# Re-sequencing the first hundred microseconds of a fused attention and MoE kernel

## Chip, cores, metric

The kernel runs on one NeuronCore of one Trainium2 chip. The metric is device microseconds of one execution. The profile's own span is 1.7 to 2.5 us shorter than the time of the same execution (median 1.8). Ratios come from timed runs. A ratio is the mean time of one kernel's fast runs over that of the other's in the same rounds, so it is not quite the ratio of the medians that are quoted beside it. A run is called slow when it is over 1.5% above the fastest run of the same kernel in its job; all others are called fast. The clock is the share of full speed that PE was granted, as the profile records it.

Engines are named as the profile names them: PE is TensorE, DVE is VectorE, ACT is ScalarE, POOL and SP issue the DMAs, and PEld is the loading of PE's weights. Tiles whose names begin with `ps` lie in PSUM; every matmul in the profiles writes to one of them.

## The reference

Sparse attention (8 global keys, 96 local keys, exponential distance bias) for 4 batches, 8 heads, 768 positions, head size 64. The heads are concatenated and go through a two-layer MLP, which the program calls MoE:

```python
scores = q @ k.T / 8 + bias          # keep = global or (0 <= rel < 96)
a = softmax(where(keep, scores, -1e9))
x = concat_heads(a @ v)              # 3072 x 512
h = x @ w_in                         # 512 -> 2048
g = s * relu(h)**2 + b
out = g @ w_out                      # 2048 -> 512, float32
```

The constant `b` goes through `w_out` as b times the column sums of `w_out`. The kernel builds those sums with 15 DVE additions ("wsum").

## The kernel before

Work is cut into 12 granules of 256 positions, each with four units of two heads. A unit has `stage_S` (scores on PE, exp on ACT, mask multiplication on DVE) and `stage_A` (attention times v on PE, division by the row sum on DVE, into `xn`). A granule then has x transposed, the first MoE matmul in eight groups (`p1`) and the second in two row blocks (`p2`). The program is scheduled by hand (`manual_schedule`): it emits each engine's instructions in the order in which they are to run, so the order of emission is the schedule. From granule 3 on, a `step` interleaves two units with MoE work of earlier granules. The part ahead of it is written out by hand. In the profiles below, `pt` holds the exp of the scores, which the mask multiplies, and `koff` and `voff` are copies of k and v, shifted by one block and with the global keys put in, for every granule but the first of a batch.

```python
def qk_by_pe(j, h2s, evac):                # q and k of one pair of head pairs in ONE PSUM tile
    for h2 in h2s:
        ps = ps_h.tile([P, 2, GB, 2, P], BF16, tag="psh")      # tag psh has 3 buffers
        ...                                # 8 transposes, n=0 is k, n=1 is q
        for n in range(2):
            evac[n](dst, ps[:, n])         # DVE, or one DVE and one ACT
def x_by_pe(j): ...                        # 8 transposes, one ACT copy of 128x1024
def x_by_dma(j):                           # from granule X_PE on
    for i in range(GB): nc.sync.dma_start_transpose(t[:, :, ...], xn[j][:, i, :])
def warm(n): ...                           # n matmuls of zeros that fill PE's time
# ---- loads: v0, (k,q)1, v1, w_in in quarters, w_out in quarters, granules 2 and 3
warm(11); cast_first(0); qk_by_pe(0, [0]); ...
s0[1](); warm(4); stage_A(0); s1 = scores(1); stage_A(1, ps_h); run(s1); warm(2)
stage_A(2); stage_A(3, ps_h); qk_by_pe(1, evac=both); x_by_pe(0)
... run(scores(2)); make_voff(1); warm(6)
run(p1[0][0:2]) ...                        # first w_in matmul
... run(p1[1][4:8])                        # granules 0 and 1 through the first MoE matmul
for qt in range(4):                        # second MoE matmul of granule 0
    for tb in range(GB): p2_mm(0, tb, qt * nq, (qt + 1) * nq)
    run(sums[qt : qt + 1])                 # wsum additions, the other 11 follow later
p2_mm(1, 0, 0, FC // 2); run(sums[4:8]); qk_by_pe(2, [0], evac=both) ...
# ... [cut: attention of granule 2 and 3]
step(6, [], p1[2][0:2], sums[9:10] + p1[2][2:4] + sums[10:11]) ...
```

The softmax here doesn't subtract the row's maximum and nothing guards it: scores larger than these inputs give would overflow.

Of the kernel before, what the change touches and what calls it, by code (L numbers as in the profile page):

```python
# [17 lines left out]
def kernel(  # L18
# [13 lines left out]
    nc = tc.nc  # L32
# [35 lines left out]
    QK_PE = 4  # L68
    X_PE = 4
# [27 lines left out]
    def load_granule(j):  # L97
        b, g = divmod(j, NGR)
        t = nat_tile(j)
        for i in range(GB):  # L100
            for n in range(2):
                nc.gpsimd.dma_start(t[:, n, i, :, :], rows_of(srcs[n], b, g * GB + i))  # L102
        load_v(j)
# [78 lines left out]
    load_granule(1)  # L182
    for i in range(4):
        load_w_in(i, 4)
# [11 lines left out]
    for h in range(H):  # L196
        slope = float(2.0 ** (-8.0 * (h + 1) / H))
        nc.scalar.activation(tmpl[:, h, 0:3, :], base[:], ACT.Exp, scale=slope)
# [5 lines left out]
    def cast_first(h2):  # L204
        hs = slice(h2 * H // 2, (h2 + 1) * H // 2)
        for n in range(2):
            nc.vector.tensor_copy(
                nat[0][:, n, :, hs, :],
                first_f32[h2, n][:].rearrange("p h (s d) -> p s h d", s=GB),
            )  # L210
# [25 lines left out]
    def qk_by_pe(j, h2s=range(HP // 2), evac=(nc.vector.tensor_copy, nc.vector.tensor_copy)):  # L236
        b, g = divmod(j, NGR)
        t = qk_tile(b)
        for h2 in h2s:
            ps = ps_h.tile([P, 2, GB, 2, P], BF16, name="ps_t", tag="psh")  # L240
            for n in range(2):
                for i in range(GB):
                    for c in range(2):
                        hp = 2 * h2 + c
                        nc.tensor.transpose(
                            ps[:, n, i, c, :],
# [3 lines left out]
            for n in range(2):  # L250
                dst = t[:, n, g * GB : (g + 1) * GB, 2 * h2 : 2 * h2 + 2, :]
                if j == 0:
# [3 lines left out]
                        ps[:, n].rearrange("p s c (b m) -> p c b m s", b=GB),  # L256
                    )
                else:
                    evac[n](dst, ps[:, n])  # L259
# [12 lines left out]
    def make_koff(j):  # L272
        b, g = divmod(j, NGR)
        if g == 0:
# [3 lines left out]
        ko = work.tile([P, GB, HP, P], BF16, name="koff", tag="koff", bufs=2)  # L278
        nc.vector.tensor_copy(ko[:], t[:, 0, r0 : r0 + GB, :, :])
        nc.vector.tensor_copy(  # L280
            ko[:, :, :, 0:NG],
            t[:, 0, 0, :, 0:NG].unsqueeze(1).to_broadcast((P, GB, HP, NG)),
        )
        koff[j] = ko
# [15 lines left out]
    def stage_S(u):  # L300
# [18 lines left out]
        for oc, kt, qt in plan:  # L319
            for hi in range(2):  # L320
                rows = slice(hi * D, (hi + 1) * D)
                nc.tensor.matmul(  # L322
                    ps[:, hi, oc * P : (oc + 1) * P],
                    lhsT=kt[rows],
                    rhs=qt[rows],
                    start=True,
                    stop=True,
                )

        def post():  # L330
            nc.scalar.activation(pt[:, :, 0:ncol], ps[:, :, 0:ncol], ACT.Exp, scale=QSCALE)  # L331
            c0 = 0 if first else 1
# [4 lines left out]
        return [post]  # L337
# [43 lines left out]
    def x_by_pe(j):  # L381
        t = xT_tile(j)
        ps = ps_h.tile([P, KC, GT], BF16, name="ps_x", tag="psh")
        for kc in range(KC):
            for i in range(GB):
                nc.tensor.transpose(
                    ps[:, kc, i * P : (i + 1) * P],
                    xn[j][:, i, kc * P : (kc + 1) * P],
                    ident_bf[:],
                )  # L390
        nc.scalar.copy(t[:], ps[:])
# [37 lines left out]
    def split_wsum():  # L429
        nc.vector.tensor_copy(hi[:], wsum[:])  # L430
# [55 lines left out]


# [9 lines left out]
    def scores(s):  # L497
        posts = []
        if s < NU // 2:
            for u in (2 * s, 2 * s + 1):  # L500
                posts += stage_S(u)
        return posts
# [9 lines left out]
    def step(s, c0, c1, c2):  # L512
# [6 lines left out]
        if not last:  # L519
# [6 lines left out]
        stage_A(2 * s + 1)  # L526
# [8 lines left out]
    warm(11)  # L535
    cast_first(0)
    qk_by_pe(0, [0])
    cast_first(1)
    s0 = scores(0)
    s0[0]()  # L540
    qk_by_pe(0, [1], evac=both)
    s0[1]()
    warm(4)
    stage_A(0)
    s1 = scores(1)
    stage_A(1, ps_h)
    run(s1)
# [3 lines left out]
    qk_by_pe(1, evac=both)  # L551
    x_by_pe(0)
    template_rest()
    make_koff(1)
    run(scores(2))
    make_voff(1)
    warm(6)
    run(p1[0][0:2])
    s3 = scores(3)
    stage_A(4)  # L560
    stage_A(5)
    run(s3)
    run(p1[0][2:4])
    stage_A(6)
    run(p1[0][4:5])
    stage_A(7)
    run(p1[0][5:6])
    x_by_pe(1)
    run(p1[0][6:7])
    run(p1[1][0:4])  # L570
    run(p1[0][7:8])
    run(p1[1][4:8])
    nq = FC // 4
    for qt in range(4):
        for tb in range(GB):
            p2_mm(0, tb, qt * nq, (qt + 1) * nq)
        run(sums[qt : qt + 1])
    load_granule(4)
    load_granule(5)
    for tb in range(GB):  # L580
        p2_hold(0, tb)


    p2_mm(1, 0, 0, FC // 2)
    run(sums[4:8])
    qk_by_pe(2, [0], evac=both)
    p2_mm(1, 0, FC // 2, FC)
    qk_by_pe(2, [1], evac=both)
    p2_hold(1, 0)
    make_koff(2)  # L590
    run(scores(4))
    p2_mm(1, 1, 0, FC // 2)
    make_voff(2)
    s5 = scores(5)
    stage_A(8)
    stage_A(9, ps_h)
    run(s5)
    p2_mm(1, 1, FC // 2, FC)
    p2_hold(1, 1)
    stage_A(10)  # L600
    qk_by_pe(3, evac=both)
    stage_A(11)
    run(scores(6))
    run(sums[8:9])
    x_by_pe(2)
    qk_by_dma(4)
    step(6, [], p1[2][0:2], sums[9:10] + p1[2][2:4] + sums[10:11])
    qk_by_dma(5)
    step(7, p1[2][4:5], sums[11:12] + p1[2][5:7], p1[2][7:8] + sums[12:13])
    hold2 = [lambda t=t: (p2_mm(2, t), p2_hold(2, t)) for t in range(GB)]  # L610
    step(8, hold2[0:1], sums[13:14] + p1[3][0:2], sums[14:15] + p1[3][2:4])
    split_wsum()
    step(9, hold2[1:2], [emit_bvec] + p1[3][4:6], p1[3][6:8])
    late = [lambda j=j, t=t: p2_late(j, t) for j in range(3) for t in range(GB)]
# [47 lines left out]
```

## Time and profile before

| | before |
|---|---|
| time | 230.25 us (228.81 to 230.26, 3 runs), 230.0 with a fourth |
| span in the profile | 228.1 us |
| PE busy | 207.7 us |
| first w_in matmul | 18.66 us |
| first second-MoE matmul | 36.87 us |
| scores of step 13 begin | 107.74 us |

From the page of the kernel before: span, PE's busy line, and the rows of the 40 equal slices for PE, for the granted clock and for DMA (tenths).

```profile
span 228.1 us, 4835 instructions
...
PE 207.7 (91%) x1954; PEld 140.9 (62%) x1977; DVE 142.9 (63%) x345; ACT 114.3 (50%) x170; POOL 67.6 (30%) x85
...
## 2 busy tenths in 40 slices
PE   7558899978798899799899999999999999999993
...
PEclk9999999999999999999999999999999999999999
DMA  6999999999999999899999935135130220311102
```

PE is close to full in the later slices, and the clock is full in all of them. The reserve is in the first half. The table of stretches shows it. Its columns are the stretch in us, its length, then busy us and instruction count of PE, PEld, DVE, ACT and POOL, then granted clock, DMA share and GB/s.

```profile
...
0.00:17.30 17.30, 11.13 (x120) 6.55 (x121) 11.40 (x33) 10.26 (x18) 15.01 (x25) 1.00 1.45 166
17.30:36.90 19.60, 17.90 (x196) 14.90 (x192) 11.47 (x30) 13.47 (x20) 7.01 (x8) 1.00 1.40 198
36.90:60.70 23.80, 20.42 (x197) 11.50 (x198) 15.63 (x34) 11.77 (x17) 14.04 (x16) 1.00 2.62 143
60.70:107.70 47.00, 43.19 (x444) 30.58 (x447) 38.28 (x94) 27.31 (x40) 30.58 (x35) 1.00 1.84 150
107.70:220.00 112.30, 110.85 (x990) 75.66 (x1003) 64.57 (x156) 51.50 (x77) 0.94 (x2) 1.00 0.49 83
```

From 107.7 to 220 us PE works 110.85 of 112.3 us. In the four stretches before it PE is idle for 6.2, 1.7, 3.4 and 3.8 us. The list of PE's waits up to 113 us says on whom it waits (us in total, times, longest).

```profile
PE ps_av L361 <- DVE xn L370: 4.1, 6, 1.1
PE ps_s L322 <- DVE koff L280: 2.1, 2, 1.2
PE ps_s L322 <- DVE qk L254: 1.4, 1, 1.4
PE ps_av L361 <- DVE voff L295: 1.3, 2, 0.7
...
PE ps_1731 L407 <- DMA xT<-xn: 0.7, 1, 0.7
...
```

ACT's waits up to 62 us have these two lines on the shared transpose tile:

```profile
ACT qk L259 <- DVE qk L259: 6.9, 4, 2.8
...
ACT qk L254 <- DVE qk L254: 1.3, 1, 1.3
```

ACT waited for DVE to finish its half of the same tile. Last, the SP queue's timeline with the DMA transposes (start, us on the queue, what):

```profile
...
103.70 2.95 SPq L396 DMA_TRANSPOSE xT<-xn  x2
107.41 6.41 SPq L266 DMA_TRANSPOSE qk<-nat  x4
```

The pair at 103.70 us is x, and one group of PE waited 0.7 us for it (the last line of PE's waits above).

### The profile page before, as it was taken

The numbers are of one execution on the slowest core, as the hardware profiler recorded it, in microseconds if no ns is written. First come the engines' busy times: TensorE is split into PE (matmuls) and PEld (weight loads), VectorE is DVE, ScalarE is ACT, GpSimd is POOL, SyncE is SP. The second block draws the span as 40 slices with busy tenths as digits, with TensorE's granted clock in tenths as the row PEclk, the third lists the DMA queues.
The fourth block names the chain that finished last, engine by engine and source line by source line (L and its number), as shares of the span: only waits on it lengthen the run. The fifth ranks groups of instructions, "written<-read, shape, count | busy, mean of one in ns | idle before, by whom it ended". The sixth has DMA issues, their size and how long they took to land.

```text
span 228.1 us, 4835 instructions
## 1 busy us (share of the span) xinstructions
PE 207.7 (91%) x1954; PEld 140.9 (62%) x1977; DVE 142.9 (63%) x345; ACT 114.3 (50%) x170; POOL 67.6 (30%) x85
## 2 busy tenths in 40 slices
PE   7558899978798899799899999999999999999993
PEld 3346786445575657477567657756765776675841
DVE  3696736638697886979567666557585674342421
ACT  7558564255977466327374455347446532340610
POOL 8973346982199560567100000000000000000000
PEclk9999999999999999999999999999999999999999
DMA  6999999999999999899999935135130220311102
GB/s 170 136 187 206 207 204 156 154 150 111 148 135 154 124 153 87 104 198 269 194 148 170 142 67 99 71 61 126 49 82 14 68 72 3 92 46 49 46 0 92
DMA packets 106934, 27.06 MB, mean 119 GB/s; under 512 B 97696, under 2 KB 103840, under 8 KB 106912
## 3 DMA queue, kind: packets, MB, share of 16 engines
q0 software_dynamic: 74944, 13.11, 81.1%
q1 hardware_dynamic: 31968, 13.64, 31.4%
q8 instruction: 15, 0.25, 0.5%
q14 instruction: 7, 0.06, 0.1%
HBM read 27.26 MB, written 6.29 MB: 147 GB/s over the span
## 4 chain that ended last, share of the span: by engine, by line
PE 70%; DVE 12%; ACT 8%; DMA 6%; issue 2%; SPq 1%; ACTq 0%; DVEq 0%
ACT pt L331 5%; PE ps_av L361 3%; DMA xT<-xn 3%; PE ps_s L322 3%; DVE xn L370 3%; DMA first<-in_q_dram 2%; DVE pt L335 2%; PE ps_1408 L446 2%; PE ps_2307 L446 2%; PE ps_1275 L446 2%; PE ps_2651 L446 2%; PE ps_2535 L446 2%; PE ps_2419 L446 2%; PE ps_2184 L446 2%; PE ps_2075 L446 2%
## 5 line engine op out<-in xcount | busy, mean ns | idle before, releaser
L407 PEld LDWEIGHTS <-w_in_bf 128*128 128x128 bf16 x768 | 72.5, 98 | 10.5 <-DMA xT<-xn 0.8
L446 PEld LDWEIGHTS <-gT 128*128 128x128 bf16 x384 | 36.3, 98 | 41.8
L416 DVE TENSOR_TENSOR gT<-gT 128x512 bf16<-128x512 bf16 x96 | 40.3, 425 | 30.8 <-ACT gT L415 28.9
L331 ACT ACTIVATE pt<-ps_s 128x1024 bf16<-128x1024 f32 (+1 forms) x48 | 43.1, 954 | 5.6 <-PE ps_s L322 5.3
L335 DVE TENSOR_TENSOR pt<-pt,tmpl 128x1024 bf16<-128x1024 bf16 (+1 forms) x48 | 30.6, 645 | 15.4 <-ACT pt L331 14.8
L102 POOL DMA_DIRECT2D nat<-in_k_dram x22 | 19.9, 906 | 16.5 <-DMA qk<-nat 11.3
L361 PEld LDWEIGHTS <-pt 128*128 128x128 bf16 x352 | 16.2, 97 | 13.9 <-DVE xn L370 5.5
L102 POOL DMA_DIRECT2D nat<-in_q_dram x22 | 20.0, 908 | 7.2 <-DMA w_in_bf<-in_moe_w_in_dram 4.3
L370 DVE TENSOR_TENSOR xn<-ps_av,rc 128x256 bf16<-128x256 f32 x45 | 19.1, 424 | 1.5
L322 PE MATMUL ps_s<-qk 64*128 64x128 bf16 x224 | 12.7, 218 | 3.3 <-DVE qk L254 1.4
L108 POOL DMA_DIRECT2D vb_89<-in_v_dram x12 | 10.6, 893 | 14.3 <-PE ps_av L361 9.9
L361 PE MATMUL ps_av<-voff,pt 128*128 128x65 bf16 x124 | 11.9, 193 | 1.3 <-DVE voff L295 1.3
L108 POOL DMA_DIRECT2D vb_88<-in_v_dram x12 | 10.9, 931 | 5.7 <-DMA w_out_bf<-in_moe_w_out_dram 3.0
L322 PEld LDWEIGHTS <-qk 64*128 64x128 bf16 x224 | 7.5, 94 | 7.8 <-issue 6.0
L361 PE MATMUL ps_av<-vb_89,pt 128*128 128x65 bf16 x112 | 9.0, 193 | 2.5 <-DVE xn L370 2.5
L361 PE MATMUL ps_av<-vb_88,pt 128*128 128x65 bf16 x96 | 8.2, 194 | 2.6 <-DVE xn L370 1.6
L322 PE MATMUL ps_s<-qk,koff 64*128 64x128 bf16 x128 | 8.0, 216 | 2.1 <-DVE koff L280 2.1
L424 DVE TENSOR_TENSOR wsum<-wsum,w_out_bf 128x512 f32<-128x512 f32 x14 | 9.6, 687 | 0.2
L369 DVE RECIPROCAL rc<-ps_av 128x4 f32<-128x4 f32 x45 | 7.9, 176 | 2.0 <-PE ps_av L361 2.0
L147 PE MATMUL ps_w<-idle 128*128 128x512 bf16 x21 | 6.9, 468 | 1.2 <-DVE idle L141 1.2
L259 ACT COPY qk<-ps_t 128x512 bf16<-128x512 bf16 x6 | 3.3, 588 | 6.9 <-DVE qk L259 6.9
L322 PEld LDWEIGHTS <-koff 64*128 64x128 bf16 x128 | 4.8, 94 | 2.4 <-DVE koff L280 2.4
(298 smaller groups left out, 327.9 us busy)
## 6 DMA issues: line engine op xcount, KB each, us to landing
out_dram<-o_sb SPq DMA_DIRECT2D x18, 256.0 KB, 2.0
nat<-in_k_dram POOLq DMA_DIRECT2D x22, 128.0 KB, 7.7
nat<-in_q_dram POOLq DMA_DIRECT2D x22, 128.0 KB, 7.5
w_in_bf<-in_moe_w_in_dram POOLq DMA_DIRECT2D x4, 512.0 KB, 10.8
w_out_bf<-in_moe_w_out_dram POOLq DMA_DIRECT2D x4, 512.0 KB, 17.7
vb_88<-in_v_dram POOLq DMA_DIRECT2D x12, 128.0 KB, 6.4
vb_89<-in_v_dram POOLq DMA_DIRECT2D x12, 128.0 KB, 8.7
out_dram<-o_early SPq DMA_DIRECT2D x6, 256.0 KB, 7.2
```

Of the source, the lines that this page charges most:

```text
L102: nc.gpsimd.dma_start(t[:, n, i, :, :], rows_of(srcs[n], b, g * GB + i))
L108: nc.gpsimd.dma_start(vbuf[b % 2][:, sb, :, 0:D], rows_of(v, b, sb))
L322: nc.tensor.matmul(ps[:, hi, oc * P : (oc + 1) * P], lhsT=kt[rows], rhs=qt[rows], start=True, stop=True,)
L331: nc.scalar.activation(pt[:, :, 0:ncol], ps[:, :, 0:ncol], ACT.Exp, scale=QSCALE)
L335: nc.vector.tensor_tensor(pv, pv, m.rearrange("p h a c -> p h (a c)"), ALU.mult)
L361: nc.tensor.matmul(av[:, i, hi, 0 : D + 1], lhsT=pt[:, hi, c * P : (c + 1) * P], rhs=vv, start=(n == 0), stop=(n == len(terms) - 1),)
L369: nc.vector.reciprocal(rc[:], av[:, :, :, D : D + 1])
L370: nc.vector.tensor_tensor(xn[j][:, :, 2 * hp * D : (2 * hp + 2) * D].rearrange("p i (h d) -> p i h d", d=D), av[:, :, :, 0:D], rc[:].to_br ...
L407: nc.tensor.matmul(ps[:, i, :], lhsT=w_in_bf[:, kc, fc * P : (fc + 1) * P], rhs=xT[j][:, kc, :], start=(kc == 0), stop=(kc == KC - 1),)
L416: nc.vector.tensor_tensor(gs, gs, gs, ALU.mult)
L424: nc.vector.tensor_tensor(wsum[:], a_, w_out_bf[:, i, :], ALU.add)
L446: nc.tensor.matmul(po[:], lhsT=gT[j][:, fc, tb * P : (tb + 1) * P], rhs=w_out_bf[:, fc, :], start=(fc == 0), stop=(fc == FC - 1),)
```

## The change

The intent is to fill PE's idle time ahead of the regular steps. The diff, cut to its core:

```diff
-    QK_PE = 4
-    X_PE = 4
+    QK_PE = 5                 # q, k and x of granule 4 by PE, not by DMA transpose
+    X_PE = 5
-    load_granule(1)
-    for i in range(4):
+    load_qk(1)
+    load_w_in(0, 4)           # first quarter of w_in ahead of v of granule 1
+    load_v(1)
+    for i in range(1, 4):
         load_w_in(i, 4)
     def qk_by_pe(...):
-            ps = ps_h.tile([P, 2, GB, 2, P], BF16, name="ps_t", tag="psh")
             for n in range(2):
+                ps = ps_h.tile([P, GB, 2, P], BF16, name="ps_t", tag="psh")
                 ...
-            for n in range(2): evac[n](dst, ps[:, n])
+                evac[n](dst, ps[:])            # x_by_pe likewise: a tile for DVE, a tile for ACT
+    def qk_wide(j, n, evac): ...               # all heads of q or of k in one tile, granules 2 to 4
     # stage_S: scores in two parts; exp and mask can be emitted apart
-    warm(4) ... warm(6)                        # ten of 23 filler matmuls go
+    # 15 wsum additions between p1 groups of granules 0/1 and the p2 of granule 0
+    p2_mm(1, 0, 0, FC // 2); scores(4); p2_mm(1, 0, FC // 2, FC); scores(5); stage_A(8) ...
+    stage_A(9, ps_h) ...                       # more attention outputs in a second PSUM buffer
+    # granule 3: scores and attention between p1 groups of granule 2
-    run(p2[NJ - 1])
+    moe_p2(NJ - 1, 0)
+    moe_p2_cols(NJ - 1, 1, 2)                  # last row block leaves in two column halves
# [cut: step order of granules 3 and 4, split_wsum's copy on ACT, template exps in two batches]
```

More of the change, by code (lines that the diff above doesn't have):

```diff
@@ L97, in load_granule, with load_qk @@
     def load_granule(j):
+        load_qk(j)
+        load_v(j)
+    def load_qk(j):
         b, g = divmod(j, NGR)
@@ L102, in load_granule @@
                 nc.gpsimd.dma_start(t[:, n, i, :, :], rows_of(srcs[n], b, g * GB + i))
-        load_v(j)
     def load_v(j):
@@ L195, with template @@
     tmpl = const.tile([P, H, 5, P], BF16, name="tmpl")
-    for h in range(H):
-        slope = float(2.0 ** (-8.0 * (h + 1) / H))
-        nc.scalar.activation(tmpl[:, h, 0:3, :], base[:], ACT.Exp, scale=slope)
+    def template(hs):
+        for h in hs:
+            slope = float(2.0 ** (-8.0 * (h + 1) / H))
+            nc.scalar.activation(tmpl[:, h, 0:3, :], base[:], ACT.Exp, scale=slope)
     def template_rest():
@@ L202, in template_rest, with cast_first @@
         nc.vector.tensor_copy(tmpl[:, :, 4, :], tmpl[:, :, 1, :])
-    def cast_first(h2):
+    def cast_first(h2, ns=(0, 1)):
         hs = slice(h2 * H // 2, (h2 + 1) * H // 2)
-        for n in range(2):
+        for n in ns:
             nc.vector.tensor_copy(
@@ L245, in qk_by_pe @@
                         nc.tensor.transpose(
-                            ps[:, n, i, c, :],
+                            ps[:, i, c, :],
                             nat[j][:, n, i, 2 * hp : 2 * hp + 2, :],
@@ L249, in qk_by_pe @@
                         )
-            for n in range(2):
                 dst = t[:, n, g * GB : (g + 1) * GB, 2 * h2 : 2 * h2 + 2, :]
@@ L255, in qk_by_pe, with qk_wide @@
                         dst.rearrange("p b c (m s) -> p c b m s", s=GB),
-                        ps[:, n].rearrange("p s c (b m) -> p c b m s", b=GB),
+                        ps[:].rearrange("p s c (b m) -> p c b m s", b=GB),
                     )
                 else:
-                    evac[n](dst, ps[:, n])
+                    evac[n](dst, ps[:])
+    def qk_wide(j, n, evac):
+        b, g = divmod(j, NGR)
+        t = qk_tile(b)
+        ps = ps_h.tile([P, GB, HP, P], BF16, name="ps_t", tag="psh")
+        for i in range(GB):
+            for hp in range(HP):
+                nc.tensor.transpose(
+                    ps[:, i, hp, :], nat[j][:, n, i, 2 * hp : 2 * hp + 2, :], ident_bf[:]
+                )
+        evac(t[:, n, g * GB : (g + 1) * GB, :, :], ps[:])
     def qk_by_dma(j):
@@ L269, in qk_by_dma, with make_koff @@
                 )
-    def make_koff(j):
+    def make_koff(j, h2=None):
         b, g = divmod(j, NGR)
@@ L277, in make_koff @@
         t = qk_tile(b)
-        ko = work.tile([P, GB, HP, P], BF16, name="koff", tag="koff", bufs=2)
-        nc.vector.tensor_copy(ko[:], t[:, 0, r0 : r0 + GB, :, :])
+        if j not in koff:
+            koff[j] = work.tile([P, GB, HP, P], BF16, name="koff", tag="koff", bufs=2)
+        ko = koff[j]
+        hs = slice(0, HP) if h2 is None else slice(2 * h2, 2 * h2 + 2)
+        nc.vector.tensor_copy(ko[:, :, hs, :], t[:, 0, r0 : r0 + GB, hs, :])
         nc.vector.tensor_copy(
-            ko[:, :, :, 0:NG],
-            t[:, 0, 0, :, 0:NG].unsqueeze(1).to_broadcast((P, GB, HP, NG)),
+            ko[:, :, hs, 0:NG],
+            t[:, 0, 0, hs, 0:NG].unsqueeze(1).to_broadcast((P, GB, len(range(*hs.indices(HP))), NG)),
         )
-        koff[j] = ko
     def make_voff(j):
@@ L318, in stage_S, with mm, expo, mask @@
             ]
-        for oc, kt, qt in plan:
-            for hi in range(2):
-                rows = slice(hi * D, (hi + 1) * D)
-                nc.tensor.matmul(
-                    ps[:, hi, oc * P : (oc + 1) * P],
-                    lhsT=kt[rows],
-                    rhs=qt[rows],
-                    start=True,
-                    stop=True,
-                )
-        def post():
+        def mm(part):
+            for oc, kt, qt in plan[part * GB : (part + 1) * GB]:
+                for hi in range(2):
+                    rows = slice(hi * D, (hi + 1) * D)
+                    nc.tensor.matmul(
+                        ps[:, hi, oc * P : (oc + 1) * P],
+                        lhsT=kt[rows],
+                        rhs=qt[rows],
+                        start=True,
+                        stop=True,
+                    )
+        def expo():
             nc.scalar.activation(pt[:, :, 0:ncol], ps[:, :, 0:ncol], ACT.Exp, scale=QSCALE)
+        def mask():
             c0 = 0 if first else 1
@@ L335, in post @@
             nc.vector.tensor_tensor(pv, pv, m.rearrange("p h a c -> p h (a c)"), ALU.mult)
-        return [post]
+        return mm, [expo, mask]
     def stage_A(u, pool=None):
@@ L379, in xT_tile, with x_by_pe @@
         return xT[j]
-    def x_by_pe(j):
+    def x_by_pe(j, evac=(nc.vector.tensor_copy, nc.scalar.copy)):
         t = xT_tile(j)
-        ps = ps_h.tile([P, KC, GT], BF16, name="ps_x", tag="psh")
-        for kc in range(KC):
-            for i in range(GB):
-                nc.tensor.transpose(
-                    ps[:, kc, i * P : (i + 1) * P],
-                    xn[j][:, i, kc * P : (kc + 1) * P],
-                    ident_bf[:],
-                )
-        nc.scalar.copy(t[:], ps[:])
+        nk = KC // len(evac)
+        for e, ev in enumerate(evac):
+            ps = ps_h.tile([P, nk, GT], BF16, name="ps_x", tag="psh")
+            for kc in range(nk):
+                for i in range(GB):
+                    c = (e * nk + kc) * P
+                    nc.tensor.transpose(
+                        ps[:, kc, i * P : (i + 1) * P], xn[j][:, i, c : c + P], ident_bf[:]
+                    )
+            ev(t[:, e * nk : (e + 1) * nk, :], ps[:])
     def x_by_dma(j):
@@ L429, in split_wsum @@
     def split_wsum():
-        nc.vector.tensor_copy(hi[:], wsum[:])
+        nc.scalar.copy(hi[:], wsum[:])
         nc.vector.tensor_tensor(lo[:], wsum[:], hi[:], ALU.subtract)
@@ L485, in moe_p2, with moe_p2_cols @@
         p2_out(j, tb)
+    def moe_p2_cols(j, tb, parts):
+        b, g = divmod(j, NGR)
+        t0 = b * S + g * GT + tb * P
+        w = DM // parts
+        for c in range(parts):
+            cs = slice(c * w, (c + 1) * w)
+            po = ps_h.tile([P, w], F32, name="ps_2c", tag="psh")
+            for fc in range(FC):
+                nc.tensor.matmul(
+                    po[:],
+                    lhsT=gT[j][:, fc, tb * P : (tb + 1) * P],
+                    rhs=w_out_bf[:, fc, cs],
+                    start=(fc == 0),
+                    stop=(fc == FC - 1),
+                )
+            o_sb = work.tile([P, w], F32, name="o_part", tag="o_part")
+            nc.vector.scalar_tensor_tensor(
+                out=o_sb[:],
+                in0=po[:],
+                scalar=s_bc[:],
+                in1=bvec[:, cs],
+                op0=ALU.mult,
+                op1=ALU.add,
+            )
+            nc.sync.dma_start(out[t0 : t0 + P, cs], o_sb[:])
     p1 = {j: [lambda j=j, f=f: moe_p1(j, f) for f in range(FC // 2)] for j in range(NJ)}
@@ L497, in scores, with scores1 @@
     def scores(s):
-        posts = []
-        if s < NU // 2:
-            for u in (2 * s, 2 * s + 1):
-                posts += stage_S(u)
-        return posts
+        if s >= NU // 2:
+            return []
+        mms, posts = zip(*[stage_S(u) for u in (2 * s, 2 * s + 1)])
+        for part in range(2):
+            for mm in mms:
+                mm(part)
+        return posts[0] + posts[1]
+    def scores1(u):
+        mm, post = stage_S(u)
+        mm(0)
+        mm(1)
+        return post
     def finish_granule(j):
@@ L510, in finish_granule, with step @@
             load_granule(j + 3)
-    def step(s, c0, c1, c2):
+    def step(s, c0, c1, c2, pool=None):
         j = 2 * s // HP
@@ L518, in step @@
         run(scores(s + 1))
-        if not last:
+        if not last and j not in voff:
             make_voff(j)
@@ L525, in step @@
         run(c1)
-        stage_A(2 * s + 1)
+        stage_A(2 * s + 1, pool)
         run(c2[0:1])
@@ L535 @@
     warm(11)
+    template(range(0, 6))
     cast_first(0)
-    qk_by_pe(0, [0])
+    qk_by_pe(0, [0], evac=both)
+    template(range(6, H))
     cast_first(1)
-    s0 = scores(0)
-    s0[0]()
+    e0, m0, e1, m1 = scores(0)
+    run([e0, e1, m0])
     qk_by_pe(0, [1], evac=both)
-    s0[1]()
-    warm(4)
+    m1()
+    e2, m2, e3, m3 = scores(1)
+    run([e2, e3])
     stage_A(0)
-    s1 = scores(1)
+    m2()
     stage_A(1, ps_h)
-    run(s1)
+    m3()
     warm(2)
@@ L550 @@
     stage_A(3, ps_h)
-    qk_by_pe(1, evac=both)
     x_by_pe(0)
     template_rest()
-    make_koff(1)
-    run(scores(2))
+    qk_by_pe(1, [0], evac=both)
+    make_koff(1, 0)
+    qk_by_pe(1, [1], evac=both)
+    e4, m4, e5, m5 = scores(2)
+    run([e4, e5])
+    make_koff(1, 1)
     make_voff(1)
-    warm(6)
-    run(p1[0][0:2])
-    s3 = scores(3)
+    run([m4, m5])
+    run(p1[0][0:1])
+    e6, m6 = scores1(6)
+    run(p1[0][1:2])
     stage_A(4)
-    stage_A(5)
-    run(s3)
-    run(p1[0][2:4])
+    e7, m7 = scores1(7)
@@ L564 @@
+    run([e6, e7])
+    stage_A(5, ps_h)
+    run([m6, m7])
+    run(p1[0][2:3])
     stage_A(6)
+    run(p1[0][3:4])
+    stage_A(7, ps_h)
     run(p1[0][4:5])
-    stage_A(7)
+    x_by_pe(1)
     run(p1[0][5:6])
-    x_by_pe(1)
+    run(p1[1][0:4])
+    run(sums[0:1])
+    run(p1[1][4:5])
+    run(sums[1:2])
     run(p1[0][6:7])
-    run(p1[1][0:4])
+    run(sums[2:3])
     run(p1[0][7:8])
-    run(p1[1][4:8])
-    nq = FC // 4
-    for qt in range(4):
-        for tb in range(GB):
-            p2_mm(0, tb, qt * nq, (qt + 1) * nq)
-        run(sums[qt : qt + 1])
+    p1[1][5]()
@@ L578 @@
+    run(sums[3:5])
+    p1[1][6]()
+    run(sums[5:6])
+    p1[1][7]()
+    run(sums[6:7])
     load_granule(4)
     load_granule(5)
-    for tb in range(GB):
-        p2_hold(0, tb)
+    p2_mm(0, 0)
+    run(sums[7:11])
+    p2_hold(0, 0)
+    p2_mm(0, 1)
+    run(sums[11:])
+    p2_hold(0, 1)
+    qk_wide(2, 0, nc.vector.tensor_copy)
+    qk_wide(2, 1, nc.scalar.copy)
+    make_koff(2)
+    make_voff(2)
+    split_wsum()
     p2_mm(1, 0, 0, FC // 2)
-    run(sums[4:8])
-    qk_by_pe(2, [0], evac=both)
+    e8, m8, e9, m9 = scores(4)
@@ L587 @@
+    run([e8, e9])
     p2_mm(1, 0, FC // 2, FC)
-    qk_by_pe(2, [1], evac=both)
+    s5 = scores(5)
+    run([m8, m9])
+    stage_A(8)
     p2_hold(1, 0)
-    make_koff(2)
-    run(scores(4))
-    p2_mm(1, 1, 0, FC // 2)
-    make_voff(2)
-    s5 = scores(5)
-    stage_A(8)
     stage_A(9, ps_h)
     run(s5)
-    p2_mm(1, 1, FC // 2, FC)
+    p2_mm(1, 1, 0, FC // 2)
+    stage_A(10)
+    qk_wide(3, 0, nc.vector.tensor_copy)
+    stage_A(11, ps_h)
+    p2_mm(1, 1, FC // 2, FC // 2 + 6)
+    qk_wide(3, 1, nc.scalar.copy)
@@ L599 @@
+    x_by_pe(2)
+    p2_mm(1, 1, FC // 2 + 6, FC)
     p2_hold(1, 1)
-    stage_A(10)
-    qk_by_pe(3, evac=both)
-    stage_A(11)
     run(scores(6))
-    run(sums[8:9])
-    x_by_pe(2)
-    qk_by_dma(4)
-    step(6, [], p1[2][0:2], sums[9:10] + p1[2][2:4] + sums[10:11])
-    qk_by_dma(5)
-    step(7, p1[2][4:5], sums[11:12] + p1[2][5:7], p1[2][7:8] + sums[12:13])
-    hold2 = [lambda t=t: (p2_mm(2, t), p2_hold(2, t)) for t in range(GB)]
-    step(8, hold2[0:1], sums[13:14] + p1[3][0:2], sums[14:15] + p1[3][2:4])
@@ L612 @@
-    split_wsum()
-    step(9, hold2[1:2], [emit_bvec] + p1[3][4:6], p1[3][6:8])
-    late = [lambda j=j, t=t: p2_late(j, t) for j in range(3) for t in range(GB)]
-    step(10, p2[3][0:1], late[0:2], late[2:3])
-    step(11, p2[3][1:2], late[3:4] + p1[4][0:2], late[4:6] + p1[4][2:4])
-    step(12, p1[4][4:5], p1[4][5:7], p1[4][7:8])
+    run(p1[2][0:3])
+    stage_A(12)
+    stage_A(13, ps_h)
+    run(scores(7))
+    run(p1[2][3:5])
+    qk_wide(4, 0, nc.vector.tensor_copy)
+    qk_wide(4, 1, nc.scalar.copy)
@@ new lines, with rest @@
+    make_koff(4)
+    qk_by_dma(5)
+    run(p1[2][5:6])
+    stage_A(14)
+    stage_A(15, ps_h)
+    run(p1[2][6:8])
+    finish_granule(3)
+    run(scores(8))
+    make_voff(4)
+    p2_mm(2, 0, 0, FC // 2)
+    emit_bvec()
+    late = [lambda j=j, t=t: p2_late(j, t) for j in range(2) for t in range(GB)]
+    def rest(j, tb):
+        p2_mm(j, tb, FC // 2, FC)
+        p2_out(j, tb)
+    step(8, [lambda: rest(2, 0)], p1[3][0:2], p1[3][2:4])
+    step(9, p2[2][1:2], p1[3][4:6], p1[3][6:8])
+    step(10, p2[3][0:1], [], late[0:2], ps_h)
@@ L618 @@
+    step(11, [lambda: p2_mm(3, 1, 0, FC // 2)], late[2:3] + p1[4][0:2], late[3:4] + p1[4][2:4])
+    step(12, [lambda: rest(3, 1)], p1[4][4:6], p1[4][6:8])
     step(13, p2[4][0:1], p1[5][0:2], p1[5][2:4])
```

## The prediction

> **What bounds it now.** In the page's engine table TensorE (PE) is busy 207.7 of 228.1 us. By stretches: 107.7 to 220 us has 110.9 busy of 112.3, so the later part is PE-bound and the change cannot shorten it. The reserve is in the opening: PE idle is 6.2 us before 17.3 us, 1.7 in 17.3-36.9, 3.4 in 36.9-60.7, 3.8 in 60.7-107.7. The list of PE's waits names them: attention-value on DVE's xn (4.1 us, one ps_av buffer), scores on koff (2.1), on the first qk evictions (2.5), on voff (1.3), on masks (1.3), x by DMA once (0.7). Also 12 of the 23 filler matmuls stand where the timeline shows gaps being filled (8.7, 11.8, 17.4 us).
>
> **What the change does.**
> 1. Each transpose tile is split so VectorE and ScalarE evict from different tiles. Today ScalarE's qk copies (0.59 us) wait 6.9 us in four cases for VectorE's (0.42). [...] ScalarE's copy at 9.65 us begins as VectorE's at 8.93 ends. Gain on the chain: about 0.4-0.7 us per pair, three or four pairs.
> 2. w_in's first quarter goes ahead of v of granule 1. The load queue's waits end on w_in at 17.6, 20.8, 23.3, 26.2 us and on w_out from 28.4 to 36; only the first comes earlier, by roughly 1 us. The other quarters still gate the first MoE pass, so this part gains little.
> 3. Ten filler matmuls go (about 0.22-0.26 us each, 2.4 us in all, 1.9 of it on the chain).
> 4. All 15 wsum additions (0.69 us each) move into 27-43 us, where VectorE is about half busy. That takes some 7 us of VectorE out of 48-83 us, where it is busiest and PE waits for xn.
> 5. koff/voff of granule 2 are made behind the second p2 block; scores and attention of granule 2 run between p2 halves; more attention outputs use a second PSUM buffer. The 3.4 us of idle in 36.9-60.7 should mostly vanish.
> 6. Granule 4's q/k and x move to PE: 24 more transposes at about 0.06 us, +1.4 us of PE, plus two 1 us ScalarE copies. It removes four DMA transposes of 6 us each, off the path.
> 7. The last tile leaves in two halves: the last eviction (0.75 us) about halves, -0.35 us.
>
> **Walk through PE's program with these durations (estimates):** first w_in matmul 18.7 -> about 17.0 us; granules 0 and 1 through the first MoE matmul 36.9 -> 35.5; first MoE matmul of granule 2 60.7 -> about 55 (two score groups and one attention less done by then, 0.7 us); scores of step 13 107.7 -> about 99-101; tail -0.35. ScalarE is nearly full at 54-63 us, so I keep 1-2 us for new stalls. The span falls by about 7 us, 228.1 -> 221; runs lie 1.5-2 us above the profiled span.
>
> **Predicted: 222.8 us, 219 to 227 in 8 of 10; faster by over 2% 0.83, within 2% 0.16, slower 0.01.**
>
> **Signs.** Right: ScalarE's wait for VectorE on qk gone; no waits for koff, voff, xT by DMA; PE busy total about 1 us lower, idle before 110 us down from 15 to about 8-9; busy per later step unchanged (8.1 us). Wrong: first w_in matmul not earlier; new PE waits on ScalarE (gT, qk, pt) at 54-63 us; PE waiting at 20-24 us for w_in or masks; wsum delaying gT squares or holding p2.
>
> **What would break it.** Without fillers, PE's own clock could fall back (128x512 fillers took 0.43 us apart at first, 0.22-0.26 later), costing 1-2 us; three shared PSUM buffers for more tiles could block; the load stream (DMA over 90% busy to 137 us) could be the limit.

## The result, and the profile after

The changed kernel took 222.75 us (221.69 to 227.79, 4 runs). The ratio of fast runs is 0.9679, 95% interval 0.9615 to 0.9743. The profiled run was fast and ran at full clock.

The same part of the page, of the kernel after:

```profile
span 219.8 us, 4920 instructions
...
PE 207.7 (94%) x2007; PEld 142.4 (65%) x2007; DVE 145.0 (66%) x350; ACT 113.8 (52%) x170; POOL 67.9 (31%) x85
...
## 2 busy tenths in 40 slices
PE   7567999999999899999999999999999999999993
...
PEclk9999999999999999999999999999999999999999
DMA  5999999999999999999999333242310311211102
```

The same stretches, kernel after:

```profile
...
0.00:17.30 17.30, 11.93 (x132) 6.87 (x133) 12.29 (x38) 11.58 (x20) 15.40 (x26) 1.00 1.45 166
17.30:36.90 19.60, 18.21 (x188) 14.75 (x183) 15.32 (x37) 12.56 (x20) 6.84 (x8) 1.00 1.41 199
36.90:60.70 23.80, 23.13 (x250) 14.96 (x249) 19.32 (x43) 15.02 (x21) 14.07 (x17) 1.00 2.37 138
60.70:107.70 47.00, 45.94 (x483) 31.82 (x481) 36.26 (x89) 26.81 (x38) 31.63 (x36) 1.00 1.86 164
107.70:220.00 112.30, 108.45 (x968) 73.96 (x966) 61.84 (x149) 47.87 (x72) 0.00 (x0) 1.00 0.39 76
```

PE's idle time in the first four stretches fell from 6.2, 1.7, 3.4 and 3.8 us to 5.4, 1.4, 0.7 and 1.1. The waits up to 113 us, kernel after:

```profile
PE ps_442 L430 <- DMA w_in_bf<-in_moe_w_in_dram: 1.2, 1, 1.2
...
PE ps_s L342 <- DVE qk L260: 0.9, 1, 0.9
PE ps_av L383 <- DVE xn L392: 0.8, 1, 0.8
PE ps_s L342 <- ACT qk L260: 0.7, 1, 0.7
...
PE ps_s L342 <- DVE koff L300: 0.2, 1, 0.2
```

The waits on voff and on x by DMA are gone, koff is down to 0.2 us, and xn is down from 4.1 to 0.8. The largest of the first 113 us is new: the second quarter of w_in, 1.2 us. (A wait of 1.2 us at the very start stands in both lists and is left out here.) ACT's waits for q and k tiles, up to 62 us, no longer name DVE. It now waits for PE's transposes:

```profile
ACT qk L276 <- PE ps_t L273: 3.7, 3, 3.2
...
ACT qk L265 <- PE ps_t L252: 0.5, 1, 0.5
ACT qk L260 <- PE ps_t L252: 0.3, 1, 0.3
```

Five marks in the traces split the gain. All are starts of PE instructions (for a step, of the scores that open it), except the end of the last matmul and the span.

| trace | first w_in | first second-MoE | step 13 | step 14 | last matmul ends | span |
|---|---|---|---|---|---|---|
| before | 18.66 | 36.87 | 107.74 | 116.59 | 224.21 | 228.1 |
| after | 16.06 | 34.46 | 100.50 | 108.47 | 216.15 | 219.8 |

The segments between marks make up the 8.3 us: the opening gave 2.41 us (36.87 to 34.46), the middle 4.83 (70.87 to 66.04), step 13 gave 0.88 (8.85 to 7.97), the rest lost 0.06 (107.62 to 107.68), and the tail gave 0.24 (3.89 to 3.65).

That trace is the best case, however. The four executions had spans of 219.8, 220.1, 221.3 and 226.0 us at mean granted clocks of 1.000, 0.998, 0.981 and 0.977. The kernel before spreads less: in 33 runs of the three later jobs its clock was 0.984 to 1.000 (one run of 33 under 0.990) and its span 226.9 to 230.4 us. The experiments had to explain both the gain and this spread.

### The profile page after: what moved, and what is told of

Read it like the earlier page. It is cut to its first block, busy times and chain, and to the rows that moved or that the text cites. A ratio compares the mean times of both kernels' runs of the same rounds, so it can differ in the third digit from the quotient of the medians.

```text
span 219.8 us, 4920 instructions
## 1 busy us (share of the span) xinstructions
PE 207.7 (94%) x2007; PEld 142.4 (65%) x2007; DVE 145.0 (66%) x350; ACT 113.8 (52%) x170; POOL 67.9 (31%) x85
## 4 chain that ended last, share of the span: by engine, by line
PE 69%; DMA 11%; POOL 7%; DVE 6%; issue 2%; SPq 2%; ACT 1%; POOLq 0%; DVEq 0%
DMA nat<-in_k_dram 5%; DMA w_in_bf<-in_moe_w_in_dram 4%; POOL nat L106 4%; PE ps_s L342 3%; PE ps_av L383 3%; DVE wsum L447 3%; SPq L283 2%; POOL vb_88 L111 2%; PE ps_1503 L469 2%; PE ps_2206 L469 2%; PE ps_2673 L469 2%; PE ps_2557 L469 2%; PE ps_2329 L469 2%; PE ps_2097 L469 2%; PE ps_1966 L469 2%
## 5 line engine op out<-in xcount | busy, mean ns | idle before, releaser
L469 PEld LDWEIGHTS <-gT 128*128 128x128 bf16 x368 | 34.4, 98 | 39.2
L392 DVE TENSOR_TENSOR xn<-ps_av,rc 128x256 bf16<-128x256 f32 x39 | 16.6, 425 | 1.3
L342 PE MATMUL ps_s<-qk 64*128 64x128 bf16 x224 | 10.6, 218 | 1.6 <-DVE qk L260 0.9
L383 PE MATMUL ps_av<-voff,pt 128*128 128x65 bf16 x108 | 10.2, 193 | 0.0
L383 PE MATMUL ps_av<-vb_89,pt 128*128 128x65 bf16 x96 | 7.8, 193 | 0.8 <-DVE xn L392 0.8
L391 DVE RECIPROCAL rc<-ps_av 128x4 f32<-128x4 f32 x39 | 6.8, 175 | 0.7 <-PE ps_av L383 0.7
L383 PE MATMUL ps_av<-vb_88,pt 128*128 128x65 bf16 x84 | 6.7, 193 | 0.6 <-DVE pt L357 0.6
L342 PE MATMUL ps_s<-qk,koff 64*128 64x128 bf16 x128 | 6.4, 216 | 0.3 <-DVE koff L300 0.2
L150 PE MATMUL ps_w<-idle 128*128 128x512 bf16 x13 | 4.8, 532 | 1.2 <-DVE idle L144 1.2
L411 PE MATMUL ps_x<-ident_bf,xn 128*128 128x128 bf16 x40 | 4.0, 220 | 1.1 <-DVE xn L392 0.5
L276 ACT COPY qk<-ps_t 128x1024 bf16<-128x1024 bf16 x3 | 3.0, 1012 | 3.7 <-PE ps_t L273 3.7
```

The source lines that it names most:

```text
L342: nc.tensor.matmul(ps[:, hi, oc * P : (oc + 1) * P], lhsT=kt[rows], rhs=qt[rows], start=True, stop=True,)
L383: nc.tensor.matmul(av[:, i, hi, 0 : D + 1], lhsT=pt[:, hi, c * P : (c + 1) * P], rhs=vv, start=(n == 0), stop=(n == len(terms) - 1),)
L391: nc.vector.reciprocal(rc[:], av[:, :, :, D : D + 1])
L392: nc.vector.tensor_tensor(xn[j][:, :, 2 * hp * D : (2 * hp + 2) * D].rearrange("p i (h d) -> p i h d", d=D), av[:, :, :, 0:D], rc[:].to_br ...
L469: nc.tensor.matmul(po[:], lhsT=gT[j][:, fc, tb * P : (tb + 1) * P], rhs=w_out_bf[:, fc, :], start=(fc == 0), stop=(fc == FC - 1),)
```

## The experiments

Each kernel is the changed one with the edit shown, unless said otherwise. The marks of all traces:

| trace | half clock in the opening | first w_in | first second-MoE | step 13 | step 14 | last matmul ends | span |
|---|---|---|---|---|---|---|---|
| e1_opening_only | 6.83 us | 17.39 | 35.54 | 106.78 | 116.16 | 223.79 | 227.6 |
| e2_later_only | 3.41 | 20.19 | 38.39 | 104.84 | 114.91 | 222.59 | 226.2 |
| e3_after_again | 6.83 | 16.96 | 35.64 | 101.75 | 110.70 | 218.38 | 222.0 |
| e4_late_sums | 6.83 | 16.85 | 35.47 | 106.24 | 114.83 | 222.50 | 226.1 |
| e8_shared_tile | 6.83 | 17.99 | 36.08 | 102.08 | 114.27 | 221.93 | 225.5 |
| e9_x5_pe | 3.41 | 16.61 | 35.23 | 103.03 | 111.00 | 218.66 | 221.9 |
| e10_gap_fill_x5_pe | none | 16.31 | 34.53 | 102.52 | 110.49 | 218.15 | 221.4 |
| e11_x5_shared_tile | 6.83 | 18.63 | 36.87 | 104.76 | 112.73 | 220.38 | 223.6 |
| e12_x5_qk4_by_dma | 6.83 | 17.14 | 35.92 | 103.13 | 111.10 | 218.76 | 222.2 |

The profiles of e5, e6 and e7 fell in slow runs. Theory: the gain is the sum of the opening and the middle, each carried to the end by a PE-bound rest. Rivals are named with each run.

### The two halves, and the change once more

e1 keeps the new opening up to the last `p1` of granule 1 with the old rest. e2 keeps the old opening with the new rest, and has the wsum additions early. e3 is the changed kernel, unedited, on the same chip.

```diff
 # e1: new opening, then
-    run(sums[0:1]) ... ; p2_mm(0, 0); run(sums[7:11]) ...      (new rest)
+    for qt in range(4): ... run(sums[qt : qt + 1]) ...         (old rest, old helpers)
 # e2: the other way round, old opening with warm(11), warm(4), warm(2), warm(6)
```

> The new opening (up to the last first-MoE matmul of granules 0 and 1) with the old rest, wsum additions at their old places. Theory: the opening is worth what it gained at the first second-MoE matmul (36.9 to 34.5 us), and the later part carries it through: profiled span about 225.7 us (225.2 to 226.4), ratio to before 0.988 to 0.993. Rival: the loads or the old middle give it back, span 227.5 or more, ratio above 0.996.

Measured: 229.94 us median, ratio 1.0002 (0.9974 to 1.0029), span 227.6. The number of the rival.

> The old opening, fillers included, with the new rest and the wsum additions early. Theory: the larger part of the gain is here, about 5.5 to 6 us: span about 222.4 us (221.7 to 223.2), ratio 0.970 to 0.978, first second-MoE matmul still near 36.9 us. Rival: the new middle needs the earlier opening (evictions, koff, loads), then less than 4 us: span above 224.

Measured: 228.78 us median, ratio 0.9981 (0.9939 to 1.0022), span 226.2. Again the rival's number.

> Control: the changed kernel on the chip of the two halves. Ratio 0.964 to 0.972; the sum of the gains of the two halves should equal its gain within 0.7 us if they are independent.

Measured: 223.73 us median, ratio 0.9695 (0.9656 to 0.9734), as expected. The halves' gains in span, 0.5 and 1.9 us, add to 2.4 us, where the whole has 6.1 (228.1 less 222.0). They do not add. (The runs of the kernel before in that job had spans of 227.4 to 228.6 us.)

The marks say why. The middle kept its worth. From the first second-MoE matmul to step 13, e2 needs 66.45 us, against 66.04 to 66.11 with the whole change and 70.87 before. So the new middle does not need the new opening, and the rival's reason is wrong although its number came. What was lost lies in two other places.

First, the opening. In e2's trace, whose opening is the old code, the first second-MoE matmul comes at 38.39 us, 1.5 later than before. That opening had the clock at half for 3.4 us and got the second half of q's first load late (PE waited 1.4 us on its cast). In e1 and e3 the trace's clock records have a spell of 6.83 us at 0.50. Here is that stretch in the changed kernel's two profiles, first the full-clock one (after), then e3, same columns as the stretches above:

```profile
11.50:18.30 6.80, 5.38 (x74) 3.83 (x71) 6.56 (x20) 3.90 (x6) 5.53 (x8) 1.00 1.62 192
```

```profile
11.50:18.30 6.80, 5.82 (x58) 4.49 (x55) 6.23 (x19) 3.20 (x5) 5.30 (x7) 0.50 1.67 191
```

The same first group of w_in matmuls, from the timelines of PE (start, us, eight matmuls), after and then e3:

```profile
16.06 1.05 PE L430 MATMUL ps_371<-xT,w_in_bf 128*128 128x256 bf16 x8
```

```profile
16.96 1.70 PE L430 MATMUL ps<-xT,w_in_bf 128*128 128x256 bf16 x8
```

The eight matmuls take 1.70 us, where they took 1.05, and the first second-MoE matmul comes at 35.64, where it came at 34.46. In the traces that were read for it, the spells at 0.50 ahead of the kernel's end last 3.41 us (e2, e9, and e8 at 110 us), 6.83 us (e1, e3, e4, e8, e11, e12) or three times 3.41 us (e6, a slow run, in the opening). What sets that length, and why some executions of a kernel have a spell and others none, is not shown.

So e1 was 1.33 us ahead at the first second-MoE matmul, where the full-clock trace is 2.41 ahead, and the old middle (71.24 us) kept 0.96 of it.

Second, step 13 (mark to mark): 7.97 us in the trace of after, but 8.85 before, 8.95 in e3, 9.38 in e1 and 10.07 in e2. That is the wait for x of granule 5 by DMA. It is taken up again with e8 and e9.

### The wsum additions

```diff
-    run(sums[0:1]) ... run(sums[6:7])     # between p1 groups of granules 0 and 1
-    p2_mm(0, 0); run(sums[7:11]) ... run(sums[11:])
+    p2_mm(0, 0); run(sums[0:2]) ... run(sums[2:4])
+    p2_mm(1, 0, 0, FC // 2); run(sums[4:8])
+    run(scores(6)); run(sums[8:9]); run(p1[2][0:3]); run(sums[9:11]); ... run(sums[13:15])
```

> The changed kernel with the 15 wsum additions where the old kernel had them (4 in the second MoE matmul of granule 0, 4 in that of granule 1, 7 between the first-MoE groups of granule 2). Theory of the prediction: VectorE is full again at 45-66 us and PE waits for xn, masks or gT there: 1 to 3 us slower than the changed kernel, ratio 0.973 to 0.981. Rival: the second PSUM buffer for attention already took the xn waits away and VectorE is not what PE waits for: under 0.5 us, ratio within 0.002 of the changed kernel.

Measured: 231.75 us median, ratio 1.0002 (0.9947 to 1.0057); fast profile, span 226.1. It was expected 1 to 3 us slower than the changed kernel and lost 4.1 in span. The middle takes 70.77 us (35.47 to 106.24): 4.66 more than e3's 66.11, and the same as the old kernel's 70.87. PE's waits from 45 to 80 us, in e3 and then in e4:

```profile
PE ps_av L383 <- DVE xn L392: 0.9, 1, 0.9
PE ps_x L411 <- DVE xT L414: 0.5, 1, 0.5
```

```profile
PE ps_x L411 <- DVE xn L392: 2.0, 2, 1.7
PE ps_av L383 <- DVE pt L357: 1.4, 2, 1.2
...
PE ps_av L383 <- DVE xn L392: 0.4, 1, 0.4
...
```

With the additions back in DVE's queue there, PE waits longer for xn, and for masks (pt). So in this schedule nearly all of the middle's gain depends on one thing: DVE is free of 10 us of additions (15 of 0.69 us) while PE needs it. Whether early additions alone would do it in the old middle was not run, nor were the other new things of the middle (the second PSUM buffer for attention, the new order of `koff` and `voff`) taken out one by one. The timed runs lost more than the profiled one: the other two fast runs had spans of 229.2 us at the same clock of 0.985, and the ratio is 0.031 above e3's, about 7 us. No trace shows where those 3 us went.

### Fillers, weights order, weights in eighths, shared tile

```diff
 # e5_fillers_back
     m1()
+    warm(4)
     ...
     run([m4, m5])
+    warm(6)
 # e6_late_quarter: load_v(1) ahead of all four load_w_in, as before
 # e7_split_quarter
-    for i in range(1, 4): load_w_in(i, 4)
+    load_w_in(2, 8); load_w_in(3, 8)
+    for i in range(2, 4): load_w_in(i, 4)
 # e8_shared_tile: the old qk_by_pe (granules 0 and 1)
```

> The changed kernel with ten fillers put back: four ahead of the second pair of score groups (PE is idle 0.95 us there), six ahead of the first w_in matmul (about 1.3 us). Prediction: 1.9 us on the chain, span 221.5 to 222. Rival, from the trace after: PE stands 1.2 us until 20.6 us for the second quarter of w_in, so whatever happens before is slack of 1.2 us: first w_in matmul about 17.4 us, third first-MoE group still at 20.6 to 20.9 us, span 219.7 to 220.3.

Measured: 226.05 us median, ratio 0.9739 (0.9683 to 0.9795). Three of its six runs were slow (spans of 225.3 to 229.3 us), and why is not known. Its three fast runs all had a clock of 1.000 and spans of 221.9, 222.6 and 223.2 us. The changed kernel's runs at 0.998 or more had 219.4, 219.8 and 220.1. Sorted and taken in pairs, the fillers cost 2.5, 2.8 and 3.1 us at equal clock, so the slack rival is wrong: their time is on the chain. About 0.5 us of that can be the chip, since the kernel before had a mean span of 228.6 us in this job and 228.1 in e3's. (Those runs may have had other waits too; no fast profile of e5 exists to tell.)

> The changed kernel with all of w_in behind the second v again. Chain theory: the first w_in matmul moves from 16.1 to about 17.6 us and the span follows, +1.5 us. Gate theory (second quarter at 20.6 us sets the pace): span +0 to +0.5 us, 219.8 to 220.4.

Measured: 227.9 us median, ratio 0.9754 (0.9668 to 0.9841) from two fast runs; the other four were slow. The better one, at a clock of 0.982, had a span of 220.9 us; the changed kernel at 0.981 to 0.985 had 221.3 to 222.0. At equal clock no loss can be seen, but that is one run. The order of the weights is not shown to be worth anything. Whether it changes how often a run is slow stays open.

> The changed kernel with the second quarter of w_in loaded as two eighths. Gate theory: the eighth that the third group needs lands about 1.2 us earlier (19.4 us), PE's 1.2 us wait shrinks or goes, the first second-MoE matmul comes 0.5 to 1.2 us earlier and the span falls to 218.7 to 219.4. Rival: masks (VectorE, ending 21.9 us) gate the same groups just behind, so under 0.3 us.

Measured: 224.1 us median of seven runs, three of them slow; ratio 0.9658 (0.9597 to 0.9719). Its two runs at a clock of 0.998 or more had spans of 219.4 and 220.6 us, against 219.4 to 220.1. No gain: the 1.2 us wait on w_in in the trace after was not what set the pace, as the rival said. That masks stand just behind is argued, not shown.

> The changed kernel with q and k of granules 0 and 1 transposed into one shared PSUM tile per pair again. Prediction: ScalarE waits for VectorE again at three or four pairs, 0.4 to 0.7 us each, 1.2 to 2.5 us before 16 us. If that is all on the chain: span 221 to 222. Gate theory: 1.2 us of it is slack ahead of the second quarter of w_in: span 219.9 to 221.

Measured: 228.92 us median, ratio 0.9904 (0.9852 to 0.9957); fast profile, span 225.5. The loss is larger than either theory allowed. The marks put it elsewhere. Against e3 (the same 6.83 us at half clock) the first w_in matmul comes 1.03 us later and the first second-MoE matmul 0.44 later. But step 13 takes 12.19 us, where e3 has 8.95. PE's waits in e8 over the whole span, the first two of the list:

```profile
PE ps_s L343 <- ACT qk L261: 3.7, 2, 2.3
PE ps L431 <- DMA xT<-xn: 2.4, 1, 2.4
...
```

The first line is the shared tile, as predicted. The second is x of granule 5, transposed by DMA, 2.4 us late. The stretch with that wait, and the next one, in e8:

```profile
106.60:110.02 3.42, 1.17 (x11) 1.09 (x12) 0.96 (x3) 0.10 (x1) 0.00 (x0) 1.00 1.70 114
110.02:113.43 3.41, 3.41 (x23) 2.50 (x22) 1.37 (x4) 1.11 (x3) 0.00 (x0) 0.50 1.79 161
```

PE worked 1.17 of 3.42 us while it waited, and in the window after that the clock is 0.50. Here the wait seems to have been paid twice: once as 2.4 us of idle time and once as 3.41 us of matmuls at a clock of 0.50. Of the 4.2 us that step 13 takes beyond the 7.97 of the trace of after, 2.4 are the wait and most of the rest can be the half clock (half of 3.41 us is 1.7, an estimate). From the issue to the landing, x takes 2.4 us at the least, and up to 7.7 (after), 8.1 (before), 9.1 (e3) and 10.2 (e2), with medians of 2.5 to 2.8. The loads of granules 10 and 11 run at the same time: POOL issues them from 90 to 105 us in the trace after. That they are what makes x land late is the author's estimate: no run held the loads back. (In the four traces of the next section, where x of granule 5 does not go by DMA, the longest landing of x is 4.2 to 4.7 us.)

### Taking the DMA transpose of granule 5 away

Four kernels test this, all with x of granule 5 on PE, three with one more edit.

```diff
 # all four
-    X_PE = 5
+    X_PE = 6
-    step(11, ..., late[3:4] + p1[4][2:4])
+    step(11, ..., p1[4][2:3] + late[3:4] + p1[4][3:4])   # one p1 group ahead of the transposes
 # e10_gap_fill_x5_pe: fillers only where PE stands idle
     m1()
+    warm(4)
     ...
-    warm(2); stage_A(2); stage_A(3, ps_h)
+    warm(4); stage_A(2); warm(2); stage_A(3, ps_h)
 # e11_x5_shared_tile: the old qk_by_pe
 # e12_x5_qk4_by_dma
-    QK_PE = 5 ; qk_wide(4, 0, ...); qk_wide(4, 1, ...)
+    QK_PE = 4 ; qk_by_dma(4) behind x_by_pe(2)
```

> The changed kernel with x of granule 5 transposed on PE too (eight transposes more), no DMA transpose of x at 95 to 107 us. Theory: the slow executions of the changed kernel (clock 0.977, 225 to 228 us) are those in which PE waits 2 to 4 us for that DMA transpose, and its clock then halves for 3.4 us. So none are left: every run at 220 to 224.5 us, the step at 100 to 110 us takes 8.0 to 8.2 us, ratio 0.962 to 0.968 over all runs. Rival: the slow executions have another cause (the chip's state): two of six still above 225 us.

Measured: 223.94 us median (223.12 to 226.06), ratio 0.9748 (0.9694 to 0.9802). Step 13 takes 7.97 us, and it takes 7.97 in e10, e11 and e12 as well. No clock fell there in the four traces. The longest span is 224.2 us, where three of the ten runs of the changed kernel had 225.3 to 226.0. So the wait in step 13 is gone, but the ratio expected was missed, and two runs (224.96 and 226.06 us) were above the range. Nor is a clock of 0.977 by itself the sign of that wait, as the theory had it: six of the 18 runs of e9, e11 and e12 have clocks of 0.975 to 0.977 without it. Their spans are at most 4.4 us above the best of their own kernel, where those of the changed kernel at 0.976 or 0.977 are 5.9 us or more above its best. The profile of e6, a slow run, shows one thing that lowers the clock so far, three times 3.41 us at half in the opening. The edit costs more than its eight transposes: from the scores of step 12 to those of step 13, e9 takes 6.13 us as after does (96.90 to 103.03; 94.37 to 100.50), but the step before that takes 7.93 us (88.97 to 96.90), where after has 6.30 (88.07 to 94.37). PE's timeline there, in e9:

```profile
...
94.30 0.39 PE L411 MATMUL ps_x<-ident_bf,xn 128*128 128x128 bf16 x4
95.14 0.38 PE L411 MATMUL ps_x<-ident_bf,xn 128*128 128x128 bf16 x4 [0.46 <-ACT gT L438]
95.94 1.03 PE L430 MATMUL ps<-xT,w_in_bf 128*128 128x256 bf16 x8 [0.41 <-DVE xT L414]
...
```

The transposes wait for a PSUM buffer and the next MoE group waits for the evicted x, 0.9 us together.

> As the run before, with eight filler matmuls put only where PE stands idle in the opening (four at 8.3 us, two more at 10.5, two at 11.6). Theory: the half-clock stretch at 11 to 18 us that most executions of the changed kernel show comes from the fillers that went; fillers in gaps that are idle anyway keep the clock and cost nothing. So granted clock 0.995 or more in most runs, first second-MoE matmul at 34.4 to 34.9 us (35.6 with the half clock), ratio 0.957 to 0.962. Rival: the fillers delay the scores and the clock still falls: ratio as the run before or worse.

Measured: 223.07 us median, 222.68 to 223.26 in six runs, ratio 0.9689 (0.965 to 0.9728). All six runs had clocks of 0.998 or 1.000, and the first second-MoE matmul came at 34.53 us, as expected. The ratio was missed for the same 1.6 us as in e9. Here are the windows ahead of and during the drop in e3, and the comparable ones in e10:

```profile
8.08:11.49 3.41, 1.61 (x32) 1.02 (x32) 2.91 (x8) 2.65 (x4) 3.41 (x6) 1.00 2.42 155
11.49:14.90 3.41, 2.67 (x31) 2.27 (x28) 3.29 (x10) 0.65 (x2) 2.98 (x4) 0.50 1.57 193
```

```profile
7.28:10.69 3.41, 2.96 (x38) 1.55 (x36) 2.85 (x7) 2.81 (x5) 3.41 (x5) 1.00 2.38 150
10.69:14.10 3.41, 2.54 (x32) 1.44 (x32) 3.31 (x11) 0.98 (x3) 3.41 (x6) 1.00 1.63 192
```

In e3 PE worked 1.61 of 3.41 us and the clock fell in the next window. With fillers in the gaps it worked 2.96 and then 2.54, and the clock stayed. Beside e9, where clocks of 0.977 to 1.000 occur, this shows that missing fillers let the clock fall, and that fillers placed in idle gaps hold it without delaying the first second-MoE matmul (34.53 us, against 35.23 in e9). No single share of busy time can be read off as the point at which the clock falls: ahead of the five falls whose windows were read in fast profiles, PE was busy 1.52 (e1), 1.61 (e3), 1.66 (e2), 1.92 (e9) and, at 106.6 us, 1.17 (e8) of 3.41 us, but a window of e9 with 1.60 us busy and one of e2 with 1.90 were not followed by a fall. No single wait of PE in e3's opening was longer than 1.2 us.

> The shared transpose tile again, with x of granule 5 on PE. On the plain changed kernel the shared tile cost 2 per cent, but 0.4 us of it stood at the first second-MoE matmul (36.1 against 35.6 us) and 3.2 us in the step at 102 us. Theory: those 3.2 us are the wait for x by DMA, not the tile: here the shared tile costs 0.3 to 1.2 us, ratio 0.002 to 0.005 above the run with x of granule 5 on PE alone. Rival: the tile itself costs 4 us or more.

Measured: 225.45 us median, ratio 0.9792 (0.9746 to 0.9838), so 0.0044 above e9, inside what was expected, though the intervals overlap. Without that edit e8's ratio stood 0.021 above e3's (from another chip). The tile costs about 1 us (0.0044 of 230), part of which can be clock: e11's runs had 0.977 to 0.985. At equal clock in the opening, e11's trace has its first second-MoE matmul 0.95 us later than e12's (36.87 against 35.92).

> x of granule 5 on PE, but q and k of granule 4 by DMA transpose as in the kernel before. PE saves 16 transposes (about 0.9 us), ScalarE one copy of 1.0 us; four DMA transposes stand in the load stream again. Theory: they were off PE's path in the kernel before, so this is worth little: within 0.004 of the run with x of granule 5 on PE alone, on either side. Rival: the DMA transposes delay the loads of granules 5 to 7 or PE waits for them: over 1.5 us slower.

Measured: 224.1 us median, ratio 0.969 (0.9629 to 0.975), 0.0058 below e9, more than the 0.004 expected, with overlapping intervals. Most of that comes from which runs count as fast: two runs of e12 at 224.89 and 225.75 us are left out as slow beside its best of 221.34, while e9's run at 226.06 stays in. Over all six runs the means are 223.8 and 224.3 us, a difference of 0.002, inside what was expected. One pair of traces speaks for a small gain, in the segment from the first second-MoE matmul to step 13: 67.21 us, against 67.80 in e9. There, granule 4's q and k by PE cost 0.6 us of PE's path rather than saving any.

e10 has the smallest spread, and its mean of 223.0 us beats that of the changed kernel's ten runs (224.2, from other jobs). Its best run does not beat the changed kernel's best (222.7 against 221.2). On its own chip it is 3.1% faster than the kernel before.

## Why the prediction was right

**The walk through PE's program held.** At full clock it said 17.0, 35.5, about 55 and 99 to 101 us. The trace after has 16.06, 34.46, 54.52 and 100.50. The span was to be about 221 and was 219.8. The part from step 14 on was called unchanged, and is: 107.62 before, 107.63 to 107.68 in all the others.

**The idle stretch of 36.9 to 60.7 us "should mostly vanish".** It did: 3.4 to 0.7 us. Idle time up to 107.7 us was to fall from 15 to 8 or 9 us, and fell from 15.1 to 8.5. The wsum additions were named as the reason why DVE would be free, and e4 shows that without them nearly all of the middle's 4.8 us is lost.

**Fillers on the chain, 1.9 us.** Shown by e5, at 2.5 to 3.1 us with the clock equal, or about 2 to 2.6 with the difference between the chips taken off. The warning in the last paragraph came true as well: without them the mean clock is under 0.99 in seven of ten executions. The four at 0.981 to 0.985, which one spell in the opening accounts for (6.83 us at half is 0.015 of 222), have spans of 221.3 to 222.0 us against 219.4 to 220.1, about 1.8 us more. That is the upper part of the 1 to 2 us estimated, and it takes back nearly what the fillers' removal brought.

**The transpose tiles** were put at 0.4 to 0.7 us for three or four pairs, thus 1.2 to 2.8 us. Measured 1.0 us at the first w_in matmul and 0.4 at the first second-MoE matmul (e8 against e3), or 1.5 and 0.95 (e11 against e12). The wait named was the right one: ACT's waits for DVE (6.9 us in four cases before) are gone. The size fits the low end at the first w_in matmul and is too large at the end of the opening, so part of the wait seems to be absorbed in between.

**The first quarter of w_in** was called a small gain. No gain is shown. One of the signs listed as wrong did appear, PE waiting for w_in at 20 to 24 us (1.2 us until 20.6), but e7 found no gain in shortening it.

**Granule 4 on PE** was costed at +1.4 us of PE for q, k and x. Its q and k alone cost 0.6 in one pair of traces (e12).

**The tail** was put at 0.35 us. The last eviction went from 0.75 to 0.49 us, and the time behind the last matmul from 3.89 to 3.65.

**PE busy was to fall by about 1 us** and did not: 207.7 both times. The fillers' busy time fell by 2.1 us (6.9 to 4.8), and the transposes added 2.5 (7.3 to 9.8), more than the 1.4 that they were costed at.

**Two things were misjudged without hurting the number.** The wait for x by DMA was counted as gone. It is gone in one profile, and 0.5 to 2.4 us in other fast ones (e4 0.5, e3 0.8, e1 with the old rest 1.2, e2 1.9, e8 2.4). And the prediction gave one number where the changed kernel has three kinds of executions: near 219.8 us of span (full clock), near 221.7 (half clock in the opening), near 225.6 (clock 0.976 or 0.977). The median of 222.75 lies where it was put because the best case was 1 us better than the walk and half the executions are worse. That these two errors cancel to 0.05 us is luck: over all ten runs of the changed kernel the median is 223.5. That the third kind is the one with a long wait for x is supported by e8 and by e9's missing tail, and the profiles of e6 and e7, though taken in slow runs, show the same pair: a wait for x of 3.8 and 2.7 us and a clock at half from 112.0 and 110.7 us. But no profile of a changed, unedited kernel fell in it, so it is not shown.

## What to carry to other kernels

A filler matmul that looks like waste may be what keeps PE's clock up: here all six runs with fillers in the gaps (e10) had clocks of 0.998 or 1.000, where the changed kernel was under 0.99 in seven of ten. Before removing fillers, look in the trace how busy PE is around them (here the falls that were read in fast profiles came after stretches of 3.41 us with 1.17 to 1.92 us busy), and move them into real gaps rather than delete them. Move work that nobody is waiting for (here 10 us of DVE additions) out of the stretch in which another engine waits on that queue; here undoing that alone took back 4.7 us in the profiled run. When parts of a change do not add up, compare marks inside the traces, segment by segment, because a clock spell (here about 1.8 us) or one late DMA (here a wait of up to 2.4 us in a fast run) can hide a part's gain in the total.
